# A fused attention and two-layer kernel: sums of weights and activations on other engines and at other times, another order of seven products, stores and weight loads at other places in the queue

## The chip, the cores and the metric

The kernel runs on one core of a Trainium2 chip. A core has a matrix engine (TensorE, PE in the rows), VectorE (DVE), ScalarE (ACT), GpSimd (POOL) and SyncE (SP), which here only issues DMA transfers. Each engine runs its own queue of instructions in order; semaphores make one engine wait for another. The metric is the time of one execution in microseconds (us) on the device, the median of several runs.

## What is computed

Inputs are `q`, `k`, `v` (4 batches, 8 heads, 576 positions, 64 wide) and two pairs of weights (512 x 2048 and 2048 x 512). The reference, cut to what matters:

```python
scores = where(mask, scale * q @ k.T + bias, -1e9)     # window of 128 positions, causal
attn = softmax(scores)
x = (attn @ v) as 2304 tokens x 512
h = x @ moe_w_in;  g = max(h, 0) ** 2;  x = g @ moe_w_out           # layer 1
h = x @ moe2_w_in; g = h * tanh(softplus(h)); out = g @ moe2_w_out  # layer 2 (Mish)
```

All of it is float32. A product is made of three matmuls on values split into a high part (float32r) and a low part, the rest: high x high, high x low, low x high.

## The kernel before

Attention and layer 1 take the first 500 us of the profile and aren't touched by the change. After them comes layer 2, tokens in three thirds `s` = 0, 1, 2 of 768. Its first matmul is done for 24 **groups** `g` (third `s = g // 8`, piece `m = g % 8` of the 2048 wide hidden layer), each as seven products instead of eight (the Strassen-Winograd scheme): `product` runs 6 matmuls of 128x384 for each, k = 0 to 6, and VectorE adds the results (tiles `c11`, `u2`, `u3`, `c22`, `u4`, `c12`, `c21`) straight from PSUM; ScalarE applies Mish.

- **Groups 1 to 8 (the first phase).** Between the products TensorE also runs the second matmul of the third 0 for the group before (`o_chunk`, tiles `acc`, weights `vh` and `vl` from `ring2_load`), in 12 chunks of three 128x512 matmuls. Six PSUM banks hold `acc`, so that two banks are left for the products: product k + 2 waits until product k has been read. `t_prepare(g - 1, k)` makes sums of the second layer's weights for later: `tb` = vh + vl at k = 0, four differences of 128x256 at k = 1 and 2 (all on GpSimd), casts `th` on ScalarE at k = 3 and 4, two subtractions on VectorE at k = 5, and four stores to `t2d` at k = 6. `run_jobs` puts in the splits of the next third's input (`x_prepare`: load `xb`, sums on GpSimd, casts on ScalarE, low parts `x_b`, `x_t` on VectorE).
- **Groups 9 to 15 and 17 to 23.** Only the products, with four PSUM banks. Weights of the first matmul come in a ring of two (`ring1_load`, tiles `ra`, `rb`, `rc`, `rd`, together 1.75 MB for a group), loaded for group g + 2 at the end of group g.
- **`products2(s)`, after group 15 and after group 23 (s = 1 and 2).** The second matmul of the thirds 1 and 2, again as seven products, `ORDER2`, each in 8 **blocks** `q` of nine 128x256 matmuls (tile `m`). A block needs the left operand's high part `hi` (ScalarE, issued 6 blocks ahead) and low part `lo` (VectorE, 4 blocks ahead, in five buffers), and a weight tile `tt` (DMA, 8 blocks ahead). Left operands are the four blocks of activations and the sums s1 to s4 of them. s3 and s1 are made on GpSimd during the groups (`sums3`); s2 (`sums_2`, blocks 0 to 7) and s4 (`sums_4`, blocks 8 to 15) on GpSimd inside `products2`. `combine` adds finished products on VectorE; in s = 1, `x_prepare(2)` runs as jobs at every second block from block 4 on.

Everything is scheduled by hand (`manual_schedule`): each engine's queue has the order in which the program calls it. All DMAs are issued by SP, so a store that waits for its data holds up every load behind it.

Of the kernel before, what the change touches and what calls it, by code (L numbers as in the profile page):

```python
# [18 lines left out]
P = 128  # L19
# [14 lines left out]
def two_layers(  # L34
# [1010 lines left out]
    def x_prepare(s):  # L1045
# [56 lines left out]
    def ring1_load(m, g):  # L1102
        at, parts = 0, []
        for tag, w in (("ra", 1024), ("rb", 512), ("rc", 1024), ("rd", 1024)):
            t = rp.tile([P, w], F32R, tag=tag, name=f"{tag}{g}")
            nc.sync.dma_start(out=t.bitcast(F32), in_=w1d[m, :, at : at + w])
            parts.append(t.rearrange("p (h c) -> p h c", h=2))
            at += w
        a, b, c, d = parts
        ring1[g] = {  # L1110
            "a11": a[:, :, 0:256],
            "a12": a[:, :, 256:512],
            "a22": b,
            "s1": c[:, :, 0:256],
            "s2": c[:, :, 256:512],
            "s3": d[:, :, 0:256],
            "s4": d[:, :, 256:512],
        }
# [67 lines left out]
    def o_evac(s, pair_):  # L1186
# [16 lines left out]
        nc.sync.dma_start(out=dst, in_=ev)  # L1203
# [3 lines left out]
    def t_prepare(m, k):  # L1207
        sub = ALU.subtract
        if k == 0:
            for e in range(2):  # L1210
                h, l = (t.bitcast(F32) for t in ring2[m, e])
                b = ap["c"].tile([P, DM], F32R, tag="c", name=f"tb{m}_{e}", bufs=4).bitcast(F32)
                nc.gpsimd.tensor_tensor(b, h, l, op=ALU.add)
                t_parts["b", e] = b
        elif k in (1, 2):
# [9 lines left out]
            for o, a, b in todo_:  # L1225
                nc.gpsimd.tensor_tensor(o, a, b, op=sub)
# [17 lines left out]
    blocks2, s3s, his, ts2, sums2 = {}, {}, {}, {}, {}  # L1244
# [13 lines left out]
    def sums3(s, m):  # L1258
# [7 lines left out]
        nc.gpsimd.tensor_tensor(b, b, c, op=ALU.add)  # L1266

    def sums_2(s, m):
        t = s3s[s, m]
        nc.gpsimd.tensor_tensor(t, block(s, A21, m), block(s, A11, m), op=ALU.subtract)  # L1270
# [5 lines left out]
    ORDER2 = (("s3", "t3"), ("s1", "t1"), ("s2", "t2"), ("s4", "b22"), ("a11", "b11"), ("a12", "b21"), ("a22", "t4"))  # L1276

    def left(s, q):
        n, m = divmod(q, 8)
        b = {"s1": A21, "s4": A21, "a11": A11, "a12": A12, "a22": A22}.get(ORDER2[n][0])  # L1280
        return s3s[s, m] if b is None else block(s, b, m)

    def high2(s, q):
        name = f"hi{s}_{q}"
        if q < 3:
            tag = ("st1", "st2", "st3")[q]
            hi = ap["x"].tile([P, TH], F32, tag=tag, name=name).bitcast(F32R)
# [71 lines left out]
    def combine(s, n, o):  # L1359
# [335 lines left out]
```

## Time and profile before

| | us |
|---|---|
| median of 3 runs | 897.01 (896.43 to 897.08) |
| the profiled execution | 898.25 |
| its span, first to last instruction | 895.9 |
| TensorE busy | 875.0 (98%) |
| VectorE busy | 649.5 (73%) |
| ScalarE busy | 500.8 (56%) |
| GpSimd busy | 359.4 (40%) |

The profiled execution is 1.24 us longer than the median, and 2.35 us of it lie outside the span. TensorE's busy time counts a matmul from its start to its modelled end. A matmul that stands in the pipeline until its operand comes can therefore be inside "busy"; the distance from one start to the next shows the pace.

### The profile page before, as it was taken

The page shows a single profiled execution, that of the slowest core. Times are in us where ns is not written, and L with a number is a line of the kernel's source. Part 1 is how long each engine was busy: PE and PEld are TensorE (multiplying, and loading weights), DVE is VectorE, ACT ScalarE, POOL GpSimd, SP SyncE. Part 2 cuts the span into 40 slices and gives each one's busy share as a digit, 9 for nine tenths or more (in the row PEclk, how much of TensorE's full clock was granted, in tenths as well). Part 3 has the DMA queues.
Part 4 walks back from the last instruction along what each step waited for, and adds up shares of the span by engine and source line. Part 5 has one row for each costly group of instructions (what it writes and reads, how often), then busy time and mean ns, then how long its engine had stood idle before and what let it go on. Part 6 is the DMA issues. An engine that isn't in the chain of part 4 may idle for free.

```text
span 895.9 us, 15580 instructions
## 1 busy us (share of the span) xinstructions
PE 875.0 (98%) x5074; PEld 770.3 (86%) x5074; DVE 649.5 (73%) x1320; ACT 500.8 (56%) x1177; POOL 359.4 (40%) x387
## 2 busy tenths in 40 slices
PE   8999999999999999999999999999989989999998
PEld 5588889998888788888888888888889979999898
DVE  6899997645798979977767445668535899455975
ACT  7888788775665666646555533344323646133542
POOL 4311145654665666532022225448112753022900
PEclk9999999999999999999999999999989999999999
DMA  8366685745685669755779676876688858685676
GB/s 297 96 218 205 206 299 175 250 142 166 228 263 181 200 214 328 248 171 189 248 251 343 253 249 223 287 274 223 213 305 320 300 175 283 195 286 196 193 237 206
DMA packets 115903, 209.11 MB, mean 233 GB/s; under 512 B 13808, under 2 KB 59248, under 8 KB 115824
## 3 DMA queue, kind: packets, MB, share of 16 engines
q1 hardware_dynamic: 115824, 208.12, 69.8%
q8 instruction: 41, 0.67, 0.3%
q14 instruction: 38, 0.31, 0.1%
HBM read 158.79 MB, written 49.28 MB: 232 GB/s over the span
## 4 chain that ended last, share of the span: by engine, by line
PE 78%; DVE 12%; DMA 4%; issue 2%; ACT 2%; SPq 1%; POOL 0%; DVEq 0%; POOLq 0%; ACTq 0%
PE h L562 17%; PE p L1139 16%; PE m L1326 13%; PE o L594 6%; PE o L590 6%; PE o L591 6%; PE o L500 3%; PE acc L1184 2%; PE acc L1183 2%; PE acc L1182 2%; DMA vl<-w2d 1%; PE pt L424 1%; DVE wf L109 1%; PE sc L329 1%; PE sc L328 1%
## 5 line engine op out<-in xcount | busy, mean ns | idle before, releaser
L1326 PE MATMUL m<-tt,hi 128*128 128x256 f32 x672 | 122.7, 283 | 0.2
L590 PE MATMUL o<-g,wh 128*128 128x512 f32 (+1 forms) x320 | 118.5, 377 | 0.0
L591 PE MATMUL o<-g,wl 128*128 128x512 f32 (+1 forms) x320 | 115.9, 369 | 0.0
L1326 PEld LDWEIGHTS m<-tt,hi 128*128 128x128 f32 x672 | 104.4, 191 | 0.7 <-issue 0.5
L1326 PE MATMUL m<-tt,lo 128*128 128x256 f32 x336 | 98.9, 294 | 4.0 <-DVE lo L1303 3.7
L629 ACT ACTIVATE r<-h 128x512 f32<-128x512 f32 (+1 forms) x80 | 44.2, 552 | 80.6 <-PE h L562 76.9
L460 POOL TENSOR_SCALAR_AFFINE_SELECT pT<-p 128x128 f32<-128x128 f32 (+2 forms) x80 | 53.9, 695 | 79.0 <-ACT p L448 78.8
L648 DVE TENSOR_TENSOR g<-gg,g 128x512 fp32r<-128x512 f32 (+1 forms) x80 | 64.0, 799 | 29.8 <-ACT g L643 21.2
L562 PE MATMUL h<-xh,wh 128*128 128x512 f32 (+1 forms) x320 | 81.5, 376 | 0.0
L594 PE MATMUL o<-g,wh 128*128 128x512 f32 (+1 forms) x320 | 79.5, 370 | 0.3
L562 PE MATMUL h<-xl,wh 128*128 128x512 f32 (+1 forms) x320 | 79.0, 369 | 0.0
L562 PE MATMUL h<-xh,wl 128*128 128x512 f32 (+1 forms) x320 | 78.8, 368 | 0.0
L1528 ACT ACTIVATE a<-c 128x384 f32<-128x384 f32 x64 | 33.5, 526 | 80.3 <-DVE c L1567 42.7
L258 POOL TENSOR_TENSOR ulo<-uraw,uhi 128x256 fp32r<-128x256 f32 (+1 forms) x48 | 47.0, 979 | 69.4 <-ACT uhi L257 46.8
L1326 PEld LDWEIGHTS m<-tt,lo 128*128 128x128 f32 x336 | 64.0, 191 | 10.1 <-DVE lo L1303 9.7
L590 PEld LDWEIGHTS o<-g,wh 128*128 128x128 f32 x320 | 60.5, 189 | 9.8 <-issue 0.5
L591 PEld LDWEIGHTS o<-g,wl 128*128 128x128 f32 x320 | 60.4, 189 | 9.3
L382 ACT ACTIVATE p<-p,st 128x128 f32<-128x128 f32 (+1 forms) x144 | 59.1, 413 | 13.6 <-DVE st L367 13.3
L594 PEld LDWEIGHTS o<-g,wh 128*128 128x128 f32 x320 | 56.5, 189 | 11.7 <-DVE g L648 1.7
L1265 POOL TENSOR_TENSOR s<-a,a 128x384 f32<-128x384 f32 x16 | 16.6, 1037 | 124.4 <-ACT a L1528 124.4
L562 PEld LDWEIGHTS h<-xl,wh 128*128 128x128 f32 x320 | 56.9, 189 | 10.5
L562 PEld LDWEIGHTS h<-xh,wl 128*128 128x128 f32 x320 | 56.9, 189 | 10.1
(149 smaller groups left out, 2152.6 us busy)
## 6 DMA issues: line engine op xcount, KB each, us to landing
wraw<-in_w SPq DMA_DIRECT2D x64, 512.0 KB, 4.6
tt<-t2d SPq DMA_DIRECT2D x64, 256.0 KB, 4.0
ra<-w1d SPq DMA_DIRECT2D x24, 512.0 KB, 5.9
rc<-w1d SPq DMA_DIRECT2D x24, 512.0 KB, 5.5
rd<-w1d SPq DMA_DIRECT2D x24, 512.0 KB, 6.2
tt<-w2d SPq DMA_DIRECT2D x48, 256.0 KB, 3.2
uraw<-in_qkT SPq DMA_DIRECT2D x24, 320.0 KB, 4.5
uraw<-in_qkT SPq DMA_DIRECT2D x24, 256.0 KB, 5.1
```

The source lines that it names most:

```text
L258: sub(u.lo[:, 0 : u.nk], u.raw[:, 256:n], u.hi[:, 256:n].bitcast(F32), op=ALU.subtract)
L382: nc.scalar.activation(probs(i, s), probs(i, s), AF.Exp, bias=u.st[:, s : s + 1], scale=-1.0, accum_out=u.st[:, sums + s : sums + 1 + s],)
L460: nc.gpsimd.affine_select(out=u.pT[:, 0:heads, k : 2 * n : 2, :][:, :, a:], in_=p[:, 0:heads, a:n], pattern=[[0, heads * (n - a)], [0, P / ...
L562: nc.tensor.matmul(ph[:, 0:n], w[:, c * P : (c + 1) * P], xs[j, c][k][:, 0:n], start=t == 0, stop=t == len(terms) - 1,)
L590: nc.tensor.matmul(o, wh[:, ws], g[:, 0, r], start=start, stop=False)
L591: nc.tensor.matmul(o, wl[:, ws], g[:, 0, r], start=False, stop=False)
L594: nc.tensor.matmul(o, wh[:, ws], g[:, 1, r], start=False, stop=stop)
L629: nc.scalar.activation(r[:, 0:n], ph[:, 0:n], AF.Relu)
L648: nc.vector.tensor_tensor(g[:, 1, 0:n], gg[:, 0:n], g[:, 0, 0:n].bitcast(F32), op=ALU.subtract)
L1139: nc.tensor.matmul(ps, w[:, z, c * P : (c + 1) * P], t[c], start=n == 0, stop=n == 5)
L1326: nc.tensor.matmul(o[c], a, b, start=m == 0 and z == 0 and c in o[3], stop=m == 7 and z == 2 and c in o[4],)
L1528: nc.scalar.activation(a[:, e, :], u, AF.Mish)
```

## The change

It does five things.

- **Sums of weights** (`t_prepare`, k = 0 to 2) go from GpSimd to VectorE: 48 instructions in groups 1 to 8, two of 128x512 and four of 128x256 a group.
- **Stores a group later.** The four stores to `t2d` of a group, and the six stores of the third 0's output after group 8, go into a list that is issued at k = 3 of the next group.
- **Weight tiles one by one.** `ring1_load` loads one tile at a time: `ra` after k = 1, `rc` after k = 4, `rd` after k = 5, `rb` after k = 6, where the buffer's last reader has just run. Group 9 now uses two PSUM banks, as groups 1 to 8 do, and not four.
- **Sums of activations.** s2 is made beside s3 and s1 in `sums3`, in the groups, on GpSimd (a third instruction of 128x384 a group). s4 goes to VectorE, at blocks 9 to 16. The input sums of the third 2 (8 instructions in `x_prepare(2)`) go to VectorE, and these jobs run at odd blocks from 17 on.
- **Order of the seven products**: s2, s3, a11, s1, a12, s4, a22 instead of s3, s1, s2, s4, a11, a12, a22, so that `combine` has 8 pairs of additions and 2 copies instead of 10 and 3.

```diff
@@ x_prepare, sums @@
+                eng = nc.vector if s == 2 else nc.gpsimd
+                eng.tensor_tensor(t, b[x, c], b[y, c], op=ALU.subtract)
...
+    def ring1_load(m, g, tag):
+        at, w, names = RING1[tag]
+        t = rp.tile([P, w], F32R, tag=tag, name=f"{tag}{g}")
+        nc.sync.dma_start(out=t.bitcast(F32), in_=w1d[m, :, at : at + w])
...
@@ product @@
-        pool, tag = banks[turns["p"] % (2 if 0 < g < 9 else 4)]
+        pool, tag = banks[turns["p"] % (2 if 0 < g < 10 else 4)]
...
@@ o_evac @@
-        nc.sync.dma_start(out=dst, in_=ev)
+        later.append((dst, ev))
...
@@ t_prepare @@
-                nc.gpsimd.tensor_tensor(b, h, l, op=ALU.add)
+                nc.vector.tensor_tensor(b, h, l, op=ALU.add)
...
-                nc.gpsimd.tensor_tensor(o, a, b, op=sub)
+                nc.vector.tensor_tensor(o, a, b, op=sub)
...
-                    nc.sync.dma_start(out=dst.rearrange("k p c -> p k c"), in_=halves(src))
+                    later.append((dst.rearrange("k p c -> p k c"), halves(src)))
...
+    def store_later():
+        while later:
+            dst, src = later.pop(0)
+            nc.sync.dma_start(out=dst, in_=src)
...
@@ sums3 @@
+        nc.gpsimd.tensor_tensor(t, b, a, op=ALU.subtract)
...
-    def sums_4(s, m):
-        t = block(s, A21, m)
-        nc.gpsimd.tensor_tensor(t, block(s, A12, m), s3s[s, m], op=ALU.subtract)
+    def sums4(s, m):
+        t = s3s[s, m]
+        nc.vector.tensor_tensor(t, block(s, A12, m), s2s[s, m], op=ALU.subtract)
...
@@ products2 @@
-        for q in range(3, 6):
+        for q in range(2, 6):
             high2(s, q)
+        low2(s, 2)
         low2(s, 3)
...
-                if q < 8:
-                    sums_2(s, q)
-                elif q < 16:
-                    sums_4(s, q - 8)
...
+                if 9 <= q < 17:
+                    sums4(s, q - 9)
...
-                if s == 1 and q >= 4 and q % 2 == 0:
+                if s == 1 and q >= 17 and q % 2:
                     run_jobs(1)
...
@@ the loop over groups and k @@
-            if 0 < g < 9:
+            if 0 < g < 9 and k < 6:
                 t_prepare(g - 1, k)
...
+            if g + 2 < 24 and k in (1, 4, 5, 6):
+                ring1_load((g + 2) % 8, g + 2, ("ra", "rc", "rd", "rb")[max(k - 3, 0)])
+            if 1 < g < 10 and k == 3:
+                store_later()
...
-        if g + 2 < 24:
-            ring1_load((g + 2) % 8, g + 2)
```

SP's queue from the end of group 8 on, before (the digits behind a name are its group, so `ra10` is the tile that group 10's first product reads):

```order
L1203 DMA out_x<-ev1_0_0_7465 128x2x512
L1203 DMA out_x<-ev1_0_1_7469 128x2x512
L1198 DMA out_x<-ev1_0_2_7473 64x512 x4
L1240 DMA t2d_97<-th7_0_7412 128x2x256
L1240 DMA t2d_97<-t2_7_0_7379 128x2x256
L1240 DMA t2d_97<-th7_1_7432 128x2x256
L1240 DMA t2d_97<-t2_7_1_7380 128x2x256
L1106 DMA ra10_7484<-w1d_95 128x1024
```

The same queue now, from the middle of group 8 to that of group 9:

```order
L1113 DMA ra10_7379<-w1d_95 128x1024
L1243 DMA t2d_97<-th6_0_7259 128x2x256
L1243 DMA t2d_97<-t2_6_0_7221 128x2x256
L1243 DMA t2d_97<-th6_1_7287 128x2x256
L1243 DMA t2d_97<-t2_6_1_7222 128x2x256
L1113 DMA rc10_7436<-w1d_95 128x1024
L1113 DMA rd10_7453<-w1d_95 128x1024
L1113 DMA rb10_7480<-w1d_95 128x512
L1113 DMA ra11_7506<-w1d_95 128x1024
L1243 DMA t2d_97<-th7_0_7410 128x2x256
L1243 DMA t2d_97<-t2_7_0_7375 128x2x256
L1243 DMA t2d_97<-th7_1_7434 128x2x256
```

`ra10` stood behind ten stores, six of which read what the copies after group 8 write; it now stands ahead of them, by half of group 8 and more.

VectorE at the turn from group 7 to group 8, before (`c21` is the reading of the last product's bank, `g` are low parts after Mish, `x1` low parts of the next third's input):

```order
L1235 TENSOR_TENSOR t2_6_0_7225<-t2_6_0_7225,th6_0_7261 128x512
L1235 TENSOR_TENSOR t2_6_1_7226<-t2_6_1_7226,th6_1_7285 128x512
L1578 TENSOR_TENSOR c21_7_7314<-u3_7_7251,p6_7_7307 128x384
L1168 TENSOR_TENSOR g12_7_7297<-c12_7_7294,g12_7_7297 128x384
L1076 TENSOR_TENSOR x1_t41_6966<-t4_1_1_7119,x1_t40_6965 128x384
L1168 TENSOR_TENSOR g21_7_7317<-c21_7_7314,g21_7_7317 128x384
L1556 TENSOR_TENSOR c11_8_7370<-p1_8_7363,p1_8_7351 128x384
```

The same place now:

```order
L1233 TENSOR_TENSOR t2_6_0_7221<-t2_6_0_7221,th6_0_7259 128x512
L1233 TENSOR_TENSOR t2_6_1_7222<-t2_6_1_7222,th6_1_7287 128x512
L1590 TENSOR_TENSOR c21_7_7320<-u3_7_7249,p6_7_7313 128x384
L1166 TENSOR_TENSOR g12_7_7301<-c12_7_7298,g12_7_7301 128x384
L1077 TENSOR_TENSOR x1_t41_6970<-t4_1_1_7121,x1_t40_6969 128x384
L1166 TENSOR_TENSOR g21_7_7323<-c21_7_7320,g21_7_7323 128x384
L1211 TENSOR_TENSOR tb7_0_7355<-vh7_0_7174,vl7_0_7176 128x512
L1211 TENSOR_TENSOR tb7_1_7357<-vh7_1_7178,vl7_1_7180 128x512
L1568 TENSOR_TENSOR c11_8_7366<-p1_8_7359,p1_8_7347 128x384
L1224 TENSOR_TENSOR t2_7_0_7375<-tb7_0_7355 128x256
```

Behind `c21` and the low parts there now stand two sums of weights (`tb7`) ahead of `c11`, and two more behind it.

GpSimd in `products2(1)`, before, from the last sums s2 to the first sums s4 (`t1` to `t4` are input sums of the third 2):

```order
L1270 TENSOR_TENSOR s3_1_5_7925<-a1_2_2_7742,a1_0_2_7740 128x384
L1270 TENSOR_TENSOR s3_1_6_8009<-a1_2_3_7914,a1_0_3_7912 128x384
L1067 TENSOR_TENSOR t1_2_0_8225<-xb12_2_0_8187,xb11_2_0_8185 128x384
L1067 TENSOR_TENSOR t3_2_0_8227<-xb22_2_0_8191,xb12_2_0_8187 128x384
L1270 TENSOR_TENSOR s3_1_7_8092<-a1_2_3_7914,a1_0_3_7912 128x384
L1274 TENSOR_TENSOR a1_2_0_7342<-a1_1_0_7341,s3_1_0_7501 128x384
L1067 TENSOR_TENSOR t2_2_0_8263<-xb22_2_0_8191,t1_2_0_8225 128x384
L1067 TENSOR_TENSOR t4_2_0_8265<-t2_2_0_8263,xb21_2_0_8189 128x384
L1274 TENSOR_TENSOR a1_2_0_7342<-a1_1_0_7341,s3_1_1_7585 128x384
```

VectorE in `products2(1)` now, at blocks 17 to 21 (`lo1_22` is block 22's low part, `c2` a combine):

```order
L1393 TENSOR_TENSOR c2_1_u3_8405<-m1_1_0_8240,c2_1_u2_8273 128x512
L1393 TENSOR_TENSOR c2_1_u3_8405<-m1_1_1_8241,c2_1_u2_8273 128x256
L1319 TENSOR_TENSOR lo1_22_8429<-a1_0_3_7922,hi1_22_8385 128x384
L1319 TENSOR_TENSOR lo1_23_8444<-a1_0_3_7922,hi1_23_8401 128x384
L1068 TENSOR_TENSOR t1_2_0_8446<-xb12_2_0_8410,xb11_2_0_8408 128x384
L1068 TENSOR_TENSOR t3_2_0_8448<-xb22_2_0_8414,xb12_2_0_8410 128x384
L1319 TENSOR_TENSOR lo1_24_8463<-a1_2_0_7338,hi1_24_8427 128x384
L1319 TENSOR_TENSOR lo1_25_8478<-a1_2_0_7338,hi1_25_8442 128x384
L1068 TENSOR_TENSOR t2_2_0_8480<-xb22_2_0_8414,t1_2_0_8446 128x384
L1068 TENSOR_TENSOR t4_2_0_8482<-t2_2_0_8480,xb21_2_0_8412 128x384
```

GpSimd now has nothing in these blocks, and VectorE has the sums `t1` and `t3` between the low parts 23 and 24, two blocks behind the load of `xb`.

## Rows read from the trace of the kernel before

**Rows 1.** TensorE's waits in the whole span: us in total, times, longest us

```profile
PE p L1139 <- DMA ra<-w1d: 3.9, 1, 3.9
PE m L1326 <- DVE lo L1303: 3.7, 3, 1.2
...
PE p L1139 <- DVE ev L1192: 2.0, 1, 2.0
...
PE p L1139 <- DVE c L1578: 1.4, 3, 0.7
```

**Rows 2.** timeline, TensorE, groups 8 to 11: start, us, what [idle <- releaser]

```profile
640.46 0.40 PE L1184 MATMUL acc<-vh,g 128*128 128x512 f32 x1
642.84 2.38 PE L1139 MATMUL p<-x_b,ra 128*128 128x384 f32 x12 [1.98 <-DVE ev L1192]
...
654.37 4.18 PE L1139 MATMUL p<-x_b,ra 128*128 128x384 f32 x12 [3.95 <-DMA ra<-w1d]
...
664.15 2.24 PE L1139 MATMUL p<-x_b,ra 128*128 128x384 f32 x12
...
671.43 0.85 PE L1139 MATMUL p<-x_b,ra 128*128 128x384 f32 x4
```

**Rows 3.** a window: busy PE, PEld, DVE, ACT, POOL; granted clock; DMA

```profile
654.00:656.00 2.00, 1.63 (x5) 1.66 (x6) 0.00 (x0) 0.00 (x0) 0.00 (x0) 0.50 1.02 391
```

**Rows 4.** timeline of SP (its DMA issues) at the same place

```profile
642.73 3.32 SPq L1198 DMA_DIRECT2D out_x<-ev  x4
...
648.58 0.66 SPq L1106 DMA_DIRECT2D ra<-w1d  x1
```

**Rows 5.** timelines of TensorE, VectorE, GpSimd in groups 1 to 8

```profile
512.66 1.31 PE L1139 MATMUL p<-x_b,ra 128*128 128x384 f32 x6 [0.32 <-DVE c L1573]
...
544.13 1.21 PE L1139 MATMUL p<-x_b,ra 128*128 128x384 f32 x6
...
559.82 1.20 PE L1139 MATMUL p<-x_b,ra 128*128 128x384 f32 x6
...
624.45 2.37 DVE L1235 TENSOR_TENSOR t<-t,th 128x512 f32<-128x512 f32 x2
...
638.22 1.28 DVE L1235 TENSOR_TENSOR t<-t,th 128x512 f32<-128x512 f32 x2
...
542.59 1.38 POOL L1213 TENSOR_TENSOR tb<-vh,vl 128x512 f32<-128x512 f32 x1 [1.99 <-DMA vl<-w2d]
```

**Rows 6.** timeline of TensorE, both `products2`; last, the chain's end

```profile
700.55 0.40 PE L1326 MATMUL m<-tt,hi 128*128 128x256 f32 x2
...
769.25 2.25 PE L1139 MATMUL p<-x_b,ra 128*128 128x384 f32 x12
...
827.50 0.40 PE L1326 MATMUL m<-tt,hi 128*128 128x256 f32 x2
...
885.74 7.07 PE m L1326 x57
```

**Rows 7.** timelines of VectorE, then GpSimd, in `products2`

```profile
836.62 10.37 DVE L1303 TENSOR_TENSOR lo<-a,hi 128x384 fp32r<-128x384 f32 x8
...
857.71 0.56 DVE L1303 TENSOR_TENSOR lo<-a,hi 128x384 fp32r<-128x384 f32 x1 [0.52 <-PE m L1326]
858.79 0.56 DVE L1303 TENSOR_TENSOR lo<-a,hi 128x384 fp32r<-128x384 f32 x1 [0.52 <-PE m L1326]
...
879.33 1.96 DVE L1303 TENSOR_TENSOR lo<-a,hi 128x384 fp32r<-128x384 f32 x4
...
820.66 1.01 POOL L1265 TENSOR_TENSOR s<-a,a 128x384 f32<-128x384 f32 x1 [5.18 <-ACT a L1528]
...
841.40 10.33 POOL L1274 TENSOR_TENSOR a<-a,s 128x384 f32<-128x384 f32 x8
```

**Rows 8.** timelines of SP and GpSimd: the second loads of `xb` in `products2(1)`

```profile
736.74 1.79 SPq L1061 DMA_DIRECT2D xb<-x1d  x4
...
740.98 4.57 POOL L1067 TENSOR_TENSOR t<-xb,xb 128x384 f32<-128x384 f32 x2 [11.11 <-DMA xb<-x1d]
```

More of the change, by code (lines that the diff above doesn't have):

```diff
@@ L1100, in run_jobs @@
                 f()
[L1102 to L1118, printed above, removed]
+    RING1 = {
+        "ra": (0, 1024, ("a11", "a12")),
+        "rb": (1024, 512, ("a22",)),
+        "rc": (1536, 1024, ("s1", "s2")),
+        "rd": (2560, 1024, ("s3", "s4")),
+    }
+    def ring1_load(m, g, tag):
+        at, w, names = RING1[tag]
+        t = rp.tile([P, w], F32R, tag=tag, name=f"{tag}{g}")
+        nc.sync.dma_start(out=t.bitcast(F32), in_=w1d[m, :, at : at + w])
+        t = t.rearrange("p (h c) -> p h c", h=2)
+        for n, name in enumerate(names):
+            ring1[g, name] = t[:, :, n * 256 : (n + 1) * 256]
     def ring2_load(m, g):
@@ L1197, in o_evac @@
                 src = ev[n % 2 * 64 : (n % 2 + 1) * 64, e, :]
-                nc.sync.dma_start(out=out[row : row + 64, :], in_=src)
+                later.append((out[row : row + 64, :], src))
             return
@@ L1235, in t_prepare @@
                 nc.vector.tensor_tensor(t, t, hi, op=sub)
-        else:
-            for z in range(2):
-                for part, src in enumerate((t_parts["h", z].bitcast(F32), t_parts["t", z])):
+                for part, src in enumerate((hi, t)):
                     dst = t2d[2 * z : 2 * z + 2, m, :, part * 256 : part * 256 + 256]
-                    nc.sync.dma_start(out=dst.rearrange("k p c -> p k c"), in_=halves(src))
+                    later.append((dst.rearrange("k p c -> p k c"), halves(src)))
+    later = []
+    def store_later():
+        while later:
+            dst, src = later.pop(0)
+            nc.sync.dma_start(out=dst, in_=src)
     BLK = {"11": 0, "21": 1, "12": 2, "22": 3}
     A11, A12, A21, A22 = range(4)
-    blocks2, s3s, his, ts2, sums2 = {}, {}, {}, {}, {}
+    blocks2, s2s, s3s, his, ts2, sums2 = {}, {}, {}, {}, {}, {}
     def block_tile(s, b, pair_):
@@ L1266, in sums3 @@
         nc.gpsimd.tensor_tensor(b, b, c, op=ALU.add)
[L1268 to L1276 removed]
+        if m % 2:
+            t = ap["x"].tile([P, TH], F32, tag=f"st{m // 2 + 1}", name=f"s2_{s}_{m}")
+        else:
+            t = xp.tile([P, 512], F32, tag=f"x32_{m // 2}", name=f"s2_{s}_{m}")[:, 0:TH]
+        s2s[s, m] = t
+        nc.gpsimd.tensor_tensor(t, b, a, op=ALU.subtract)
+    def sums4(s, m):
+        t = s3s[s, m]
+        nc.vector.tensor_tensor(t, block(s, A12, m), s2s[s, m], op=ALU.subtract)
+    ORDER2 = (
+        ("s2", "t2"),
+        ("s3", "t3"),
+        ("a11", "b11"),
+        ("s1", "t1"),
+        ("a12", "b21"),
+        ("s4", "b22"),
+        ("a22", "t4"),
+    )
     def left(s, q):
         n, m = divmod(q, 8)
[L1280 to L1281 removed]
+        b = {"s1": A21, "a11": A11, "a12": A12, "a22": A22}.get(ORDER2[n][0])
+        if b is None:
+            return (s2s if n == 0 else s3s)[s, m]
+        return block(s, b, m)
     def high2(s, q):
         name = f"hi{s}_{q}"
[L1285 to L1287 removed]
+        if q == 0:
+            his["first"] = gp.tile([P, 2, 512], F32R, tag="g", name=name, bufs=2)
+        if q < 2:
+            hi = his["first"][:, q, 0:TH]
         else:
@@ L1494, in two_layers @@
         if fc in (12, 14):
-            ring1_load((fc - 12) // 2, (fc - 12) // 2)
+            for tag in RING1:
+                ring1_load((fc - 12) // 2, (fc - 12) // 2, tag)
         prev = (0, j, fc)
@@ L1597, in two_layers @@
                 t_load(s, 2 * (m - 3) + (k == 4))
-            if s and m == 7 and k in (2, 4, 6):
+            if s and m == 7 and k in (2, 4):
                 high2(s, k // 2 - 1)
                 low2(s, k // 2 - 1)
+            if g + 2 < 24 and k in (1, 4, 5, 6):
+                ring1_load((g + 2) % 8, g + 2, ("ra", "rc", "rd", "rb")[max(k - 3, 0)])
+            if 1 < g < 10 and k == 3:
+                store_later()
         done()
```

47 lines of the change are left out of this document (21 added, 26 removed).

## The prediction

> **What bounds the kernel now.** I read the waits of TensorE first. The table gives TensorE 98% busy, so only its idle time and its pace can be won back. Three waits stand out [rows 1]: 3.9 us for a weight tile `ra`, 2.0 us for VectorE's copies `ev`, 3.7 us in three pieces for low parts `lo`; 1.4 us more falls on `c21` (line 1578). Then I read TensorE's timeline stage by stage, because a stretch that is "busy" can still be slow: I take the distance between two starts and compare it with the same work where nothing holds it up. That gives four losses.
>
> - *A, groups 9 and 10.* The last chunk of group 8 starts at 640.46, so group 9 was free to start 0.23 later, at 640.69; it starts at 642.84, 2.15 late. An undisturbed group takes 671.43 - 664.15 = 7.28 [rows 2]. From 642.84 to 664.15 are two groups: 21.31 - 14.56 = 6.75 lost. 3.95 of that is the wait for `ra`. The rest is what follows it: the granted clock is 0.50, the lower of its two levels (1.2 against 2.4 GHz), after TensorE stood idle [rows 3], and group 10's first two products last 4.18 instead of 2.24 [rows 2]. A = 8.9. Its cause is SP's queue: stores of `ev` and `t2d` are issued first, 3.32 us for the four small ones alone, and `ra` goes out at 648.58 [rows 4].
> - *B, groups 1 to 8.* A clean group takes 559.82 - 544.13 = 15.69 [rows 5]. From group 1's start (512.66) to 640.69 pass 128.03, against 125.52: B = 2.5. Most of it comes as VectorE reaches `c21` late behind two subtractions, 2.37 us while GpSimd runs, 1.28 when it doesn't [rows 5].
> - *C, `products2(1)`.* 700.55 to 769.25 is 68.70 [rows 6]. A clean block takes 1.08, where VectorE waits for TensorE [rows 7]; 56 blocks are 60.48. C = 8.2.
> - *D, `products2(2)`.* 827.50 to the chain's end, 885.74 + 7.07 = 892.81, is 65.31 [rows 6], so D = 4.8.
>
> C and D have one cause. While GpSimd makes its sums, eight low parts take 10.37, 1.29 each [rows 7], more than a block's 1.08, so VectorE sets the pace; alone, four of them take 1.96, 0.49 each [rows 7]. GpSimd's sums take 1.29 each there as well [rows 7]: the two engines slow each other down.
>
> **The change, part by part.** *Weight tiles one by one, stores later, two banks in group 9 (A).* `ra10` goes out in the first half of group 8, more than a group ahead of its use, and group 9 needs no bank that the copies hold. Both waits go, and the low clock with them: -8.9. Added: with two banks, a product may start only when the one before the last has been read. One reading (0.56 for that size [rows 7]) fits into the next product's 1.04; `c22` and `u4` read the same bank one behind the other, so the wait lies between 0 and another 0.56. I take 0.2, since two readings just pass 1.04. The stores fall into group 9, on the queue ahead of `rc11`: ten, at no more than 0.83 each (3.32 for four [rows 4]). So `rc11` goes out some 10.4 after group 9's start (2.1 for the first two products, 8.3 for the stores), and group 11 reads it at 16.6. `ra10` took 5.8 from issue to use amid such traffic (648.58 to 654.37), so it is covered, if barely, and I take nothing; uncovered, it is a wait as long as the load is late. A net: -8.7.
>
> *Sums of weights on VectorE (B).* A group gets two additions of 128x512, 0.64 each by the undisturbed 1.28 for two [rows 5], and four of 128x256, between 0.32 (half of that) and 0.56 (the 384-wide form): 2.6 to 3.5, I take 2.7, being nearer to half. At the same time the slowing by GpSimd goes: the two subtractions alone win 1.1 a group. In the fullest groups VectorE then has 7 readings at 0.56, 9 low parts at 0.49, 1.28 and 2.7, 12.3 of 15.7 us, and the additions fall at k = 0 to 2, ahead of `c11` and not of `c21`. They need `vl`, which was there 1.5 us ahead of the group in the tightest case (542.59 against 544.13 [rows 5]); SP no longer stands at stores for VectorE, so the loads go out earlier. Queued behind a late `vl` would be `c11`, and TensorE two products later. I expect 2.2 of the 2.5 back, with bounds of 0 and 2.5.
>
> *Sums of activations (C and D).* GpSimd does nothing in `products2` but the last three sums of piece 7, of which the third is new. VectorE alone gets 8 sums s4 and, in s = 1, 8 input sums, each 0.49, and loses two combines, two instructions of about 0.5 each. Its work in `products2(1)`: 56 low parts + 8 + 8 + 14 low parts of inputs = 86 x 0.49 = 42, and 8 combines = 8: 50 of 60.5 us. It fits, and in blocks 9 to 16 too, where two at 0.49 stand against 1.08. What stays: at the entry, hi and lo of block 2 still come after the last Mish, and for three blocks GpSimd still slows VectorE: 0.4 for the wait that is there now and 2 or 3 x 0.21, some 0.8 a stage. In D some 0.7 more stays at the end, where the last product's loop isn't touched and the drain of the last matmul counts in. D net: -3.3.
>
> C has a new wait. `t1` and `t3` now stand in VectorE's queue two blocks behind the load of `xb`. From issue to first use the load took 4.24 (736.74 to 740.98 [rows 8]); it is issued as block 17 ends. VectorE stands from about 1.6 to 4.8 after that, then waits for the last piece, which goes out 1.4 later, and reaches `lo` of block 24 at about 6.1 to 7.0 after, when TensorE needs it at 6.7. So 0 to 0.8, twice; behind the low part stand the combines and all further low parts, but VectorE has a sixth of its time to spare. I take 0.7 for both. C net: 8.2 - 0.8 - 0.7 = -6.7.
>
> *A rule beside the rows.* The rows show 1.29 for a low part beside GpSimd, less than 1.01 for GpSimd's sum while VectorE only reads PSUM, and 0.49 for the low part alone, together [rows 7]. The Trainium skill (SBUF — State Buffer, "Who interferes with whom") says that a VectorE instruction with two SBUF inputs and a GpSimd instruction that reads SBUF exclude each other, the second to start waiting for the first to finish. By it a low part would take 1.5 beside a sum, and three sums at each entry 0.6 a stage more than I take: 1.2 in the sum, 877.3. The 1.29 does not bear full exclusion out, so I keep to the row.
>
> The changed order of products by itself moves nothing on TensorE: the same matmuls, and the operands of its first product, s2, are made in the groups.
>
> **The sum**, against the profiled execution's 898.25: 8.7 + 2.2 + 6.7 + 3.3 = 20.9, so 877.35. The median lies 1.24 under the profiled execution: 876.1, I say 876.
>
> **Rivals.** *1. The input sums hold VectorE up.* If `xb` lands 8 us after its issue instead of some 4.3, TensorE waits some 4 us at each of two loads: 884. It decides from a landing of about 5 on. For: VectorE waits in order, and the weight tiles `tt` share the DMA engines. Against: the 4.24 was measured among the same tiles. *2. Traffic.* In group 9 the stores, the ring and the rest come to some 4 MB; if `rc11` or `rd11` lands late, a wait like that of `ra` returns with its low clock, 4 to 6 us: 880 to 882. Against: 6 us lie between issue and use even at 0.83 for each store. *3. Slower.* VectorE, now the one that waits for `vl` at the head of each group, holds up `c11`, and with two banks TensorE. TensorE takes no harm up to some 2.8 us behind the group's start. To turn 20.9 won into a loss over seven groups takes 3.2 us each, so a landing about 7.5 later than in the tightest case now: 900. For: [rows 5], the 1.99 wait of GpSimd for `vl`. Against: the loads now go out earlier. *4. It isn't GpSimd that slows VectorE.* Then C and D stay and VectorE has more to do: 898.25 - 1.24 - 8.7 - 2.2 = 886 or more. Against: the low parts are at 0.56 and less once GpSimd's last sum has ended, at 851.73 [rows 7].
>
> **How the numbers follow.** The forecast as worked out, with all four gains: 0.70 (872.6, if no new cost comes, 24.4 won, up to 880). Rival 1: 0.12. Rival 2: 0.11. Rival 4: 0.03. Rival 3: 0.03. Below 872.6: 0.01. For 8 in 10 the range takes the forecast's band and most of rivals 1 and 2: 872.5 to 883. A measurement of this kernel can tell about 0.2% (1.8 us) from no change. All cases but rival 3 are faster by more: 0.96; rival 3 is slower: 0.03; 0.01 for what lies between.
>
> **What would show it.** A right: TensorE has no wait for `ra` or `ev` at groups 9 and 10, and the granted clock stays at its upper level there. B: no wait for `c21`, groups at 15.69. C and D: low parts at 0.49, stages of about 62 and 62 us. C's new wait shows as VectorE waiting for the DMA `xb`, and TensorE for `lo` behind it. It is wrong if VectorE waits for `vl` at a group's head, if `rc` or `rd` makes TensorE wait in group 11, or if low parts stay at 1.29.

## The result and the profile after

The changed kernel takes 880.36 us (median of 4 runs, 878.96 to 881.81) against 896.72 of the kernel before, measured beside it: a ratio of 0.9822, 95% interval 0.9800 to 0.9843. The forecast was 876.0 with a range of 872.5 to 883.0: the time lies inside, 4.4 us above the forecast. The profiled execution took 879.86 us, its span is 878.1.

Set against each other by stage, from the starts of TensorE's instructions in the two profiled executions:

| part | before | after | gain | forecast |
|---|---|---|---|---|
| A, groups 9 and 10 | 23.46 | 14.92 | 8.54 | 8.7 |
| B, groups 1 to 8 | 128.03 | 125.62 | 2.41 | 2.2 |
| C, `products2(1)` | 68.70 | 64.58 | 4.12 | 6.7 |
| D, `products2(2)` | 65.31 | 62.93 | 2.38 | 3.3 |
| everywhere else | | | 0.4 | 0 |
| span | 895.9 | 878.1 | 17.8 | 20.9 |

A and B came as worked out; C and D gave 3.5 us less. The rows of the profile after follow in the same order.

TensorE's wait for low parts in the whole span (total, times, longest), against [rows 1]; of the others there, `ra`, `ev` and `c21` (now line 1590) are gone from the list:

```profile
PE m L1342 <- DVE lo L1319: 2.2, 3, 1.3
```

*A.* TensorE's first products of groups 9, 10 and 11 in its timeline, then a window (busy TensorE, weight loads, VectorE, ScalarE, GpSimd; granted clock; DMA share and GB/s); [rows 2, 3] of before:

```profile
637.99 2.25 PE L1137 MATMUL p<-x_b,ra 128*128 128x384 f32 x12
...
645.63 2.24 PE L1137 MATMUL p<-x_b,ra 128*128 128x384 f32 x12
...
652.91 2.24 PE L1137 MATMUL p<-x_b,ra 128*128 128x384 f32 x12
```
```profile
645.00:650.00 5.00, 5.00 (x31) 5.00 (x30) 1.76 (x5) 2.04 (x4) 3.04 (x3) 1.00 1.06 397
```

Group 9 takes 645.63 - 637.99 = 7.64 and group 10 the undisturbed 7.28. The granted clock stays at 1.00, the upper of its two levels. The 0.36 more in group 9 is what two banks cost; the forecast had 0.2. SP's queue there, against [rows 4]: `ra10` goes out at 625.97. The stores hold up `rc11`, which goes out at 649.25, but TensorE reads it only at 654.99, 5.74 later, and doesn't wait:

```profile
625.97 0.32 SPq L1113 DMA_DIRECT2D ra<-w1d  x1
...
643.40 5.76 SPq L1243 DMA_DIRECT2D out_x<-ev  x6
649.25 0.54 SPq L1113 DMA_DIRECT2D rc<-w1d  x1
```

*B.* VectorE and then TensorE in the groups 1 to 8, against [rows 5]: the two subtractions take 1.29 beside nothing on GpSimd, the new sums 1.29 for a pair and 0.42 for each small one, and TensorE's groups 15.68 (559.55 - 543.87), the clean pace. The first row of TensorE is the start of group 1, with the same short wait as before; from there to group 9 it is 637.99 - 512.37 = 125.62:

```profile
541.86 1.29 DVE L1233 TENSOR_TENSOR t<-t,th 128x512 f32<-128x512 f32 x2
...
545.23 1.29 DVE L1211 TENSOR_TENSOR tb<-vh,vl 128x512 f32<-128x512 f32 x2
...
548.42 0.42 DVE L1224 TENSOR_TENSOR t<-tb,tb 128x256 f32<-128x256 f32 x1
```
```profile
512.37 1.33 PE L1137 MATMUL p<-x_b,ra 128*128 128x384 f32 x6 [0.31 <-DVE c L1585]
...
543.87 1.20 PE L1137 MATMUL p<-x_b,ra 128*128 128x384 f32 x6
...
559.55 1.21 PE L1137 MATMUL p<-x_b,ra 128*128 128x384 f32 x6
```

*C and D.* The starts of `products2(1)`, of the product behind it and of `products2(2)`, then the end of the chain, 867.99 + 7.08 = 875.07, against [rows 6]:

```profile
689.31 0.40 PE L1342 MATMUL m<-tt,hi 128*128 128x256 f32 x2
...
753.89 2.25 PE L1137 MATMUL p<-x_b,ra 128*128 128x384 f32 x12
...
812.14 0.40 PE L1342 MATMUL m<-tt,hi 128*128 128x256 f32 x2
...
867.99 7.08 PE m L1342 x57
```

VectorE's low parts in the middle of `products2(2)`, against the 1.29 of [rows 7]: one of them, with the next 1.08 behind it. It takes 0.56 by its row, and VectorE waits 0.52 for TensorE before it, so TensorE sets the pace:

```profile
837.10 0.56 DVE L1319 TENSOR_TENSOR lo<-a,hi 128x384 fp32r<-128x384 f32 x1 [0.52 <-PE m L1342]
```

And the new wait in `products2(1)`. First SP's two issues of `xb`, then VectorE's whole wait for it (total, times, longest), VectorE at the second load, and TensorE's three waits; [rows 6, 8] of before:

```profile
710.29 1.79 SPq L1061 DMA_DIRECT2D xb<-x1d  x4
...
732.75 1.80 SPq L1061 DMA_DIRECT2D xb<-x1d  x4
```
```profile
DVE t L1068 <- DMA xb<-x1d: 8.4, 4, 4.3
```
```profile
738.31 0.56 DVE L1068 TENSOR_TENSOR t<-xb,xb 128x384 f32<-128x384 f32 x1 [4.27 <-DMA xb<-x1d]
739.23 0.56 DVE L1068 TENSOR_TENSOR t<-xb,xb 128x384 f32<-128x384 f32 x1 [0.37 <-DMA xb<-x1d]
739.71 1.02 DVE L1319 TENSOR_TENSOR lo<-s,hi 128x384 fp32r<-128x384 f32 x2
740.64 1.01 DVE L1412 TENSOR_TENSOR c_c<-m,c_c 128x512 f32<-128x512 f32 x2
741.58 0.55 DVE L1068 TENSOR_TENSOR t<-xb,t 128x384 f32<-128x384 f32 x1
742.16 0.56 DVE L1068 TENSOR_TENSOR t<-t,xb 128x384 f32<-128x384 f32 x1
742.64 1.02 DVE L1319 TENSOR_TENSOR lo<-s,hi 128x384 fp32r<-128x384 f32 x2
```
```profile
716.98 0.39 PE L1342 MATMUL m<-tt,lo 128*128 128x256 f32 x1 [0.42 <-DVE lo L1319]
...
740.31 0.39 PE L1342 MATMUL m<-tt,lo 128*128 128x256 f32 x1 [1.29 <-DVE lo L1319]
743.24 0.39 PE L1342 MATMUL m<-tt,lo 128*128 128x256 f32 x1 [0.51 <-DVE lo L1319]
```

The second load is used 5.56 us after its issue (738.31 - 732.75), and behind the two low parts a combine and two more input sums stand in a row, 2.0 us without a low part. TensorE waits once for the landing and once for that row. The distances between its starts (0.36 for three matmuls where nothing holds them up) show more than the named waits: of the 4.10 that the stage is over 60.48, some 0.9 are lost at the entry, 0.7 at the first load and 0.2 behind the combine that follows it, and 2.3 at the second load.

### The profile page after: what moved, and what is told of

Its sections match the earlier page's. It is cut to its first block, busy times and chain, and to the rows that moved or that the text cites. A ratio compares the mean times of both kernels' runs of the same rounds, so it can differ in the third digit from the quotient of the medians.

```text
span 878.1 us, 15594 instructions
## 1 busy us (share of the span) xinstructions
PE 865.5 (99%) x5074; PEld 766.6 (87%) x5074; DVE 631.7 (72%) x1384; ACT 500.5 (57%) x1173; POOL 270.5 (31%) x315
## 4 chain that ended last, share of the span: by engine, by line
PE 82%; DVE 11%; issue 2%; ACT 2%; DMA 1%; POOL 1%; DVEq 0%; SPq 0%; POOLq 0%; ACTq 0%
PE p L1137 19%; PE h L562 17%; PE m L1342 13%; PE o L594 6%; PE o L590 6%; PE o L591 6%; PE o L500 3%; PE acc L1182 3%; PE acc L1181 3%; PE acc L1180 2%; DVE wf L109 2%; DVE wl L129 1%; PE pt L424 1%; PE sc L329 1%; PE sc L328 1%
## 5 line engine op out<-in xcount | busy, mean ns | idle before, releaser
L1342 PE MATMUL m<-tt,lo 128*128 128x256 f32 x336 | 96.0, 286 | 2.5 <-DVE lo L1319 2.2
L460 POOL TENSOR_SCALAR_AFFINE_SELECT pT<-p 128x128 f32<-128x128 f32 (+2 forms) x80 | 56.3, 725 | 76.6 <-ACT p L448 76.3
L1268 POOL TENSOR_TENSOR s<-a,a 128x384 f32<-128x384 f32 x16 | 16.6, 1041 | 161.9 <-ACT a L1540 161.9
```

Source lines behind the costliest of these rows:

```text
L460: nc.gpsimd.affine_select(out=u.pT[:, 0:heads, k : 2 * n : 2, :][:, :, a:], in_=p[:, 0:heads, a:n], pattern=[[0, heads * (n - a)], [0, P / ...
L1342: nc.tensor.matmul(o[c], a, b, start=m == 0 and z == 0 and c in o[3], stop=m == 7 and z == 2 and c in o[4],)
```

## The experiments

My theory with the two profiles side by side: A and B are settled by the order of the loads and by VectorE's sums; C lost its 2.6 us to VectorE standing at the DMA of `xb`; the engines slow each other down only where both read SBUF. The rivals stand in each expectation.

**Each part alone.** `a_only` is the kernel before with one-by-one loads, later stores and two banks in group 9; `b_only` with the sums of weights on VectorE; `cd_only` with the changes inside and for `products2`.

> The kernel before with part A alone: weight tiles loaded one by one, the stores a group later, two banks in group 9. My theory (A is worth 8.5 us, by itself): ratio to before 0.9905, no wait for ra or ev in groups 9 and 10, the granted clock at its upper level there, the stages of the two last products as before (68.7 and 65.3 us). Rival (the parts need one another, since the weight sums on GpSimd still make the stores and VectorE late): ratio above 0.994, a wait for ra of over 1 us remains.

> The kernel before with only the sums of weights moved from GpSimd to VectorE. Theory: the waits for c21 (1.4 us) go and groups 5 to 8 come down to 15.7 us, 2.2 us, ratio 0.9975, since VectorE's own instructions are shorter without GpSimd beside them. Rival (VectorE then has more to do and waits for the loads vl, which still stand behind stores in SP's queue): 1.0 or above, with waits of VectorE for vl and of TensorE for c11 or c21.

> The kernel before with only the change inside and for the two last products: s2 made in the groups, s4 and the third 2's input sums on VectorE, other order of the seven products, jobs at odd blocks from 17 on. Theory: the changed kernel's gains in these two stages (4.1 and 2.4 us) come back whole: 6.5 us, ratio 0.9928, the waits for ra and ev stay. Rival (part of it was the earlier loads of the ring and the stores moved away): under 5 us.

Measured against 896.52 of before: `a_only` 887.72 (0.9903, 0.9890 to 0.9916), `b_only` 894.03 (0.9973, 0.9963 to 0.9983), `cd_only` 889.73 (0.9926, 0.9910 to 0.9943). The product of the three is 0.9803, at the lower end of the whole change's interval but inside it, so by the times the parts neither help nor hinder each other by an amount that shows. What each leaves is seen in TensorE's timeline of groups 9 and 10; first `a_only`, then `b_only`, then `cd_only`:

```profile
639.65 2.25 PE L1136 MATMUL p<-x_b,ra 128*128 128x384 f32 x12
647.32 2.25 PE L1136 MATMUL p<-x_b,ra 128*128 128x384 f32 x12
```
```profile
640.58 3.39 PE L1139 MATMUL p<-x_b,ra 128*128 128x384 f32 x12 [1.98 <-DVE ev L1192]
651.37 2.35 PE L1139 MATMUL p<-x_b,ra 128*128 128x384 f32 x12 [1.64 <-DMA ra<-w1d]
```
```profile
642.78 3.91 PE L1140 MATMUL p<-x_b,ra 128*128 128x384 f32 x12 [1.98 <-DVE ev L1193]
654.49 2.32 PE L1140 MATMUL p<-x_b,ra 128*128 128x384 f32 x12 [2.56 <-DMA ra<-w1d]
```

Both waits go with part A alone and stay with the other two. The wait for `ev` is 1.98 in each, that for `ra` 1.64 to 3.95 with that of before, so a single profile gives the second only roughly.

The groups 1 to 8 show one thing that the times don't. Of the 2.41 that B gained there, `b_only` has 1.61 (126.42 instead of 128.03) and `a_only` 0.74 (127.29). In `b_only` GpSimd still makes input sums of the next third beside the two subtractions of group 4, because their load `xb` goes out at 565.41, behind stores and all weight tiles of a group; the pair takes 2.92 at 574.15, and group 5 lasts 16.10. In the whole change `xb` goes out at 561.36, these sums are done at 572.34, before the pair begins at 573.70, and the pair takes 1.29.

`cd_only` holds four edits at once. Below, the input sums and GpSimd's reading are taken apart; what the new order of the seven products is worth by itself no run shows.

**The load of `xb` ahead of its use** (`load_ahead`): the changed kernel, in which the loads go out at blocks 16 and 33 and the sums that read them run at blocks 21 and 39.

```diff
             jobs.extend(x_prepare(2))
+            jobs[7] += jobs.pop(10)
...
-                if s == 1 and q >= 17 and q % 2:
+                if s == 1 and (q == 16 or q >= 21 and q % 2):
                     run_jobs(1)
```

> The changed kernel with the two loads of xb issued further ahead of their sums: the first at block 16 with the sums at block 21 (before: 17 and 19), the second at block 33 instead of 37, its sums at block 39 as they were. Same instructions otherwise. Theory (VectorE's wait for xb is what kept products2(1) at 64.6 us and not 62): VectorE's waits for xb go from 8.4 to under 2 us, TensorE's waits for lo behind them (2.2 us) go, the stage takes 62.0, the ratio to the changed kernel is 0.997, to before 0.979. Rival (VectorE has too much to do there, whatever it waits for): the stage stays at 64 or more.

Measured 877.43 us, 0.9790 (0.9774 to 0.9806). VectorE's wait for `xb` falls from 8.4 us to 1.1, `products2(1)` takes 61.40 (688.59 to 749.99), and TensorE's timeline shows no wait in it. VectorE's wait, then the stage's first product and the first one behind it:

```profile
DVE t L1068 <- DMA xb<-x1d: 1.1, 2, 0.8
```
```profile
688.59 0.40 PE L1342 MATMUL m<-tt,hi 128*128 128x256 f32 x2
...
749.99 2.25 PE L1137 MATMUL p<-x_b,ra 128*128 128x384 f32 x12
```

The wait, and not VectorE's work, took the 3.2 us (64.58 - 61.40): the same instructions run in both. By the times the gain is 2.9 us of medians, with intervals that just touch; the stage shows it more clearly.

**The same sums back on GpSimd** (`xsum_gp`), the other way of taking VectorE out of that wait.

```diff
-                eng = nc.vector if s == 2 else nc.gpsimd
-                eng.tensor_tensor(t, b[x, c], b[y, c], op=ALU.subtract)
+                nc.gpsimd.tensor_tensor(t, b[x, c], b[y, c], op=ALU.subtract)
```

> The changed kernel with the input sums of the third 2 on GpSimd again, the rest as changed. VectorE then doesn't wait for xb, GpSimd does, and its eight sums slow only the few low parts beside them, by some 0.7 each, which VectorE's spare time covers: products2(1) 62.0 to 62.5 instead of 64.6, ratio to the kernel before 0.980. Rival: what VectorE loses is its work and GpSimd's hold on it, not the wait: 64.6 or more, 0.982.

Measured 876.57 us, 0.9772 (0.9757 to 0.9787); `products2(1)` takes 61.53. GpSimd now stands at the load, and VectorE pays for the eight sums in a few low parts only. VectorE, then GpSimd:

```profile
716.18 2.67 DVE L1318 TENSOR_TENSOR lo<-a,hi 128x384 fp32r<-128x384 f32 x2
```
```profile
713.53 2.31 POOL L1067 TENSOR_TENSOR t<-xb,xb 128x384 f32<-128x384 f32 x2 [20.48 <-DMA xb<-x1d]
```

For this stage, then, the move of the input sums to VectorE was no gain by itself; it cost what the wait costs.

**Is it GpSimd that slows the low parts?** (`gp_read`, `gp_write`): the changed kernel with work on GpSimd that nobody reads.

```diff
+                if s == 2 and 16 <= q < 40:   # gp_read
+                    nc.gpsimd.tensor_tensor(s2s[2, 6], s2s[2, 2], s2s[2, 4], op=ALU.subtract)
...
+                if s == 2 and 16 <= q < 40:   # gp_write
+                    nc.gpsimd.memset(s2s[2, 6], 0.0)
```

> The changed kernel with 24 subtractions of 128x384 (two SBUF inputs) added on GpSimd at blocks 16 to 39 of products2(2); what they write is never read, so the output stays the reference's. My theory (the two engines slow each other down): low parts beside them take some 1.29 us instead of at most 0.56 and VectorE sets the pace again, 24 blocks at 0.2 us more each: products2(2) 62.9 + 4.8 = 67.7 us; ratio to the kernel before 0.9822 + 0.0054 = 0.988. With full exclusion (1.5 for a low part) 24 x 0.42 = 10 us: 73, ratio 0.993. Rival 4 of the prediction (it isn't GpSimd): low parts stay at 0.5, stage 62.9, ratio 0.982.

> The changed kernel with 24 memsets of 128x384 (GpSimd writes SBUF and reads nothing) added on GpSimd at blocks 16 to 39 of products2(2); what they write is never read. If it is GpSimd's reading of SBUF that holds VectorE up, low parts stay at some 0.5 us, the stage at 62.9 and the ratio to the kernel before at 0.982. If any work of GpSimd does, low parts take about 1.29 beside a memset and the stage grows by as much of 4.8 us as the memsets last.

`gp_read` takes 882.63 us, 0.9843 (0.9825 to 0.9861), and its `products2(2)` 66.11 us (811.79 to the chain's end, 857.66 + 20.24) instead of 62.93 (62.54 to 63.92 in the other kernels that leave this stage as changed). GpSimd, then VectorE (eight low parts, a combine of four instructions):

```profile
830.34 30.69 POOL L1450 TENSOR_TENSOR s<-s,s 128x384 f32<-128x384 f32 x24 [13.64 <-DVE s L1279]
```
```profile
834.25 9.59 DVE L1319 TENSOR_TENSOR lo<-a,hi 128x384 fp32r<-128x384 f32 x8
843.76 1.94 DVE L1399 TENSOR_TENSOR c_u<-m,c_u 128x512 f32<-128x512 f32 x4
```

A low part takes 9.59 / 8 = 1.20 beside GpSimd's subtraction of 1.28 (30.69 / 24), and VectorE sets the pace again. The combine, which reads one operand from PSUM, takes 1.94 beside the same work, and 1.95 in the changed kernel. `gp_write` takes 880.0 us, 0.9816 (0.9801 to 0.9831), its stage 63.25; beside its 24 memsets the low parts stay as they were (GpSimd, then one of VectorE's low parts):

```profile
830.70 11.37 POOL L1450 MEMSET s<- 128x384 f32 x24 [13.62 <-DVE s L1279]
```
```profile
837.11 0.56 DVE L1319 TENSOR_TENSOR lo<-a,hi 128x384 fp32r<-128x384 f32 x1 [0.52 <-PE m L1342]
```

So rival 4 of the prediction falls: it is GpSimd. Its work that only writes SBUF does no harm, which leaves the reading; a GpSimd instruction with a single SBUF input wasn't run. The 24 memsets were done in 11.4 us, so that this holds for that stretch only. I had expected 4.8 us more for `gp_read`; it was 3.2, as a low part took 1.20 and not 1.29.

**Which part of A does it?** `loads_end` loads the four tiles at the group's end again, with the stores a group later; `stores_now` issues the stores in their own group again, with the tiles loaded one by one.

```diff
-            if g + 2 < 24 and k in (1, 4, 5, 6):   # loads_end
-                ring1_load((g + 2) % 8, g + 2, ("ra", "rc", "rd", "rb")[max(k - 3, 0)])
...
+        if g + 2 < 24:
+            for tag in RING1:
+                ring1_load((g + 2) % 8, g + 2, tag)
...
-            if 1 < g < 10 and k == 3:   # stores_now
+            if 0 < g < 9 and k == 6:
                 store_later()
```

> The changed kernel with the four weight tiles loaded together at a group's end, as before, while the stores stay a group later. If the stores ahead of ra10 made its lateness, ra10 is issued at some 638 us, lands at most 5.8 us later, ahead of group 10's start at 645.6: no wait, ratio to the kernel before 0.982 (to 0.983). Rival: loading one by one is what removes the wait; then TensorE waits for ra again, 2 to 6 us with what follows: 0.985 to 0.989.

> The changed kernel with the stores issued at the end of their own group again, weight tiles still loaded one by one. ra10 stays ahead of the stores, so group 10 doesn't wait. But ra11 now stands behind ten stores, goes out at some 648 us, as in loads_end, and is needed at 652.9: TensorE waits 1 to 2 us for it, ratio to the kernel before 0.984. Rival: the order of the loads alone made the gain and the later stores are worth nothing: no wait, 0.982.

`loads_end`: 881.26 us, 0.9831 (0.9815 to 0.9848). Group 10 doesn't wait, but the stores are now ahead of `ra11`, which goes out at 648.22, and group 11 waits for it. TensorE at groups 10 and 11, then SP:

```profile
645.74 2.24 PE L1137 MATMUL p<-x_b,ra 128*128 128x384 f32 x12
654.41 2.32 PE L1137 MATMUL p<-x_b,ra 128*128 128x384 f32 x12 [1.23 <-DMA ra<-w1d]
```
```profile
641.60 6.53 SPq L1243 DMA_DIRECT2D out_x<-ev  x6
648.22 0.96 SPq L1113 DMA_DIRECT2D ra<-w1d  x1
```

With the stores alone moved, the wait comes a group later, and it is 1.23 where `b_only`, `cd_only` and before have 1.64 to 3.95. The time by itself can't be told from that of the whole change; the wait can. `stores_now`: 880.50 us, 0.9814 (0.9795 to 0.9832), as fast as the whole change. Here I was wrong: the stores begin as soon as `rb10` is out, so that `ra11` stands behind all ten and still goes out at 645.71, 2.5 us earlier than in `loads_end`, and group 11 starts without a wait, 7.29 behind group 10 (645.26):

```profile
639.68 5.93 SPq L1243 DMA_DIRECT2D out_x<-ev  x6
645.71 0.55 SPq L1113 DMA_DIRECT2D ra<-w1d  x1
```
```profile
652.55 2.24 PE L1137 MATMUL p<-x_b,ra 128*128 128x384 f32 x12
```

So the loads one by one are what removes the wait for `ra`; beside them, the later stores add nothing that can be measured.

**Two banks in group 9** (`banks4`): four again.

```diff
-        pool, tag = banks[turns["p"] % (2 if 0 < g < 10 else 4)]
+        pool, tag = banks[turns["p"] % (2 if 0 < g < 9 else 4)]
```

> The changed kernel with four PSUM banks in group 9 again, the rest as changed. My theory: the wait for the copies ev returns (2.0 us ahead of group 9's first product), without the wait for ra, and the 0.36 us that two banks cost in group 9 goes: +1.6 us, ratio to the kernel before 0.984. Rival: the stores behind the copies made that wait long, and with these a group later it is short: 0.982 or less.

Measured 882.56 us, 0.9849 (0.9831 to 0.9867), 2.2 us more than the changed kernel by the medians, where I had expected 1.6 and no low clock. The wait for `ev` is back at 1.98 although the stores come a group later, so the rival falls; and the low clock is back with it: 0.62 and 0.53 in the two windows of 2 us that follow it, and 3.82 us for the two products that take 2.25 otherwise. TensorE, then a window:

```profile
640.74 3.82 PE L1137 MATMUL p<-x_b,ra 128*128 128x384 f32 x12 [1.98 <-DVE ev L1190]
```
```profile
640.74:642.74 2.00, 2.00 (x7) 2.00 (x8) 0.00 (x0) 0.01 (x1) 0.00 (x0) 0.62 0.00 0
```

**The rest of C and D** (`best`): `load_ahead` with the operands of blocks 0 to 3 made ahead of the last Mish, and the last product's weight tiles loaded at blocks 8 to 36.

```diff
-            if s and m == 7 and k in (2, 4):
-                high2(s, k // 2 - 1)
-                low2(s, k // 2 - 1)
+            if s and m == 7 and 1 <= k < 5:
+                high2(s, k - 1)
+                low2(s, k - 1)
...
-        for q in range(2, 6):
+        for q in range(4, 6):
             high2(s, q)
-        low2(s, 2)
-        low2(s, 3)
...
-                if s == 2 and q == 40:
-                    t_load(s, 54)
-                    t_load(s, 55)
-                if q + 8 < (56 if s == 1 else 54):
+                if s == 2 and q % 4 == 0 and 8 <= q < 40:
+                    t_load(s, 46 + q // 4)
+                if q + 8 < (56 if s == 1 else 48):
```

> load_ahead with two more edits. (a) Entry: the high and low parts of blocks 0 to 3 are made at k = 1 to 4 of the group before, so that none stands behind the last Mish. (b) Tail: the eight weight tiles of the last product of the third 2 are loaded at blocks 8 to 36 into the ring of the first matmul, which is free by then, and not eight blocks ahead. My theory of D: the entry's 1.0 us is the order behind the last Mish, and the tail's 1.0 us a late weight tile, since that product runs through its eight tiles in 0.36 us each. Then products2(1) takes 60.6 instead of 61.4 and products2(2) 61.2 instead of 62.9: ratio to the kernel before 0.976. Rivals: the entry's loss is GpSimd's last sums beside VectorE, and stays; the tail's loss is the low parts, which stand behind the combine, and stays: 0.979 with both.

Measured 873.33 us, 0.9736 (0.9721 to 0.9751): faster than both kernels. `products2(1)` runs from 688.90 to 749.36, 60.46 us, the clean 56 x 1.08 = 60.48 but for the rounding, and `products2(2)` from 807.61 to 868.37, 60.76. In its chain of waits (start, us, engine, line) each stage is one unbroken run of matmuls:

```profile
689.06 60.47 PE m L1344 x504
...
807.77 60.60 PE m L1344 x504
```

Against `load_ahead` the entry gave 0.94 (61.40 - 60.46) in C, and entry and tail together 2.05 in D (62.81 - 60.76). The tail's part is late weight tiles. In the changed kernel no wait is recorded there, but the last product's first tiles follow each other at 0.60 to 0.69 instead of 0.36 (starts at 865.40, 866.06, 866.70, 867.39 and 867.99). In `stores_now`, whose tail is that of the changed kernel, the profile names the tile twice, here the second time:

```profile
868.26 0.48 PE L1342 MATMUL m<-tt,hi 128*128 128x256 f32 x2 [0.40 <-DMA tt<-t2d]
```

GpSimd's three last sums still run beside the first low parts in `best`; with the low parts made earlier that no longer reaches TensorE.

## Where the prediction held, and where it didn't

*A held.* The mechanism and the size: 8.54 in the profile, and 8.8 for the part alone (896.52 - 887.72), against 8.7. Of its three edits the prediction could not say which does it. The experiments do: one-by-one loads for `ra`, two banks for `ev`. The stores, on which I spent most of the working (`rc11` "if barely"), add nothing beside these two. `rc11` went out 11.3 after group 9's start, not 10.4, and was read at 17.0, not 16.6, so it was covered; two banks cost 0.36, not 0.2. Rival 2 didn't come about, but `loads_end` shows how near it is: there a tile `ra11` that goes out at 648.22 makes TensorE wait 1.23 us.

*B held in its size:* 2.41 against 2.2. The prediction counted it as won by the sums on VectorE; these give 1.61 of it by themselves, and about 0.8 comes only when part A lets the loads of `xb` out earlier, so that GpSimd's input sums no longer run beside the two subtractions. The 2.5 us by which the median of `b_only` is shorter don't tell this apart, as the wait for `ra` changes from one execution to the next. Rival 3 has nothing for it: VectorE never waits for `vl`. Its additions took 1.29 and four times 0.42, 3.0 where 2.7 was taken, inside the bounds.

*C and D: the mechanism held, two terms of what stays were too small.* The pace of 1.08 came back as forecast. The new wait of C was put at "0 to 0.8, twice", 0.7 in all; it was 3.2. Two steps of that term failed. One is "From issue to first use the load took 4.24": one row, used for both loads. The first load did take 4.13 (710.29 to 714.42), the second 5.56, beyond the point of 5 us that was named for rival 1. The other is the room that was given to it, and it weighs more. The low part behind the two sums (block 24's, at the second load block 44's) was said to be needed 6.7 after the issue; by TensorE's pace it was needed 6.1 after it (at 716.40 and 738.86), as SP issued both loads 0.6 behind the block's end. And "VectorE has a sixth of its time to spare" failed: a sixth on average is of no use where a combine and two sums stand between two low parts at the place where VectorE is already late.

The record shows how tight the place is. Seven kernels have this part as changed (`after`, the changed kernel itself, with `cd_only`, `gp_read`, `gp_write`, `banks4`, `loads_end` and `stores_now`). In each, the stage takes 52.5 us (52.49 to 52.53) plus the two times from a load's issue to the start of the second sum, which reads its last piece; in the changed kernel these are 5.61 (715.90 - 710.29) and 6.48 (739.23 - 732.75). Over the seven they run from 5.36 to 7.10 and the stages from 63.98 to 65.57. So every microsecond by which the last piece lands later comes out of TensorE's time. With the forecast's own landing, 4.24 and 1.4 more for the last piece, the sum would be 52.5 + 2 x 5.64 = 63.8, that is 2.4 lost beside the entry's 0.94, not 0.7; the longer landing adds the other 0.8. This is rival 1 in a small form. Why the landing varies isn't settled: in `stores_now` and `loads_end` it is the first load that took longer (4.87 against 4.44 to the first use, and 5.09 against 4.43).

The entry was put at 0.8 a stage, with a part for GpSimd's slowing; it is 0.94, and in C all of it goes when the first operands no longer stand behind the last Mish. The tail and the drain of D were put at 0.7, taken over from before because "the last product's loop isn't touched". They took 1.5 (2.45 lost in D, less 0.94), of which 0.28 stay in `best`. The loop wasn't touched, but its weight tiles were late, as `best` shows by loading them earlier. That they became late because the first blocks of the stage no longer run at 1.29 is argued and not shown.

*The rule weighed beside the rows held only in part.* A low part beside GpSimd's sum took 1.29 before and 1.20 in `gp_read`; alone some 0.5, and the sum alone 1.01. The Trainium skill (SBUF — State Buffer, "Who interferes with whom") says that a VectorE instruction with two SBUF inputs contends with a GpSimd instruction that reads SBUF, not with one that only writes it, and that a VectorE instruction with at most one SBUF input, outside its two-port modes, doesn't contend: the memsets and the combines of these runs agree. That the one fully blocks the other (1.5 for the pair) none of the rows shows; keeping to the row was right.

*From the sum to the time.* The sum gave 877.35 for the profiled execution; it was 879.86. C and D are 3.5 short; 0.6 came back outside the span (1.76 now, 2.35 before) and 0.4 elsewhere in it. The other 1.75 us to the distance of 4.25 (from 876.11, before rounding) are the step from one execution to the median: that of before lay 1.24 above its median, which the forecast took off again, and that of after 0.50 below its own. A single execution can't carry such a step.

## What to carry to other kernels

When an instruction is moved onto a queue that runs in order, look for what it waits for, not for what it takes: eight sums of half a microsecond fitted VectorE's free time easily, and the load behind which two of them stood cost 3.2 us, which an earlier issue gave back. A landing time from one row is a sample; cover the longest seen, up to the last piece that is read, and count the row of work that follows a late instruction, not the mean load of its engine. And a loop that isn't touched can still lose when those ahead of it change: look again at whether its loads come in time.

## What the runs showed of the hardware

- VectorE and GpSimd slow each other when both read SBUF with full operands: 1.20 to 1.29 us for a VectorE subtraction of 128x384 that takes about 0.5 alone. VectorE additions with one operand in PSUM (1.94 for four beside GpSimd, 1.95 without) and GpSimd memsets (no low part longer beside them) are free of it in these runs.
- One and the same load lands at quite different times: four pieces of 128x384 took 4.13 to 6.20 us from the issue of the first to their first use, over the two loads of the seven kernels with this part as changed.
- The same idle time doesn't always take the clock down. After the wait of 1.98 us for `ev`, group 9's first two products took 2.38 in the profile of before [rows 2], 3.39 in `b_only`, 3.91 in `cd_only` and 3.82 in `banks4`, where the granted clock was 0.62 and 0.53; in the profile of before it fell at the next wait, for `ra`, instead [rows 3]. What decides between them no run here shows.
